# Two edits to an order of work: where a delta-rule chunk reads its old state, and how weight loads and row transposes follow each other on one queue

## The chip, the core and the metric

The kernel runs on one core of a Trainium2 chip. A core has a matrix engine (TensorE, PE in the profile; PEld is its weight load), three engines for elementwise work (VectorE = DVE, ScalarE = ACT, GpSimd = POOL) and SyncE (SP), which here does nothing but issue transfers. Each engine takes its instructions in order; semaphores join the engines. The metric is the device time of one execution in microseconds (us); lower is better.

## The reference

Three stages in a row. Only what is computed matters here:

```python
# 1. delta-rule attention, 4 x 8 heads, 768 tokens, width 48
for t in range(S):
    y[:, :, t] = q[t] @ state                       # reads the old state
    v_old = k_n[t] @ state
    state = state + beta[t] * outer(k_n[t], v[t] - v_old)
# 2. dense layer on 3072 tokens of width 384:   x = leaky_relu(x @ w_in) @ w_out      (d_ff 2048)
# 3. expert layer, 8 experts, one per token:
e_idx = argmax(x @ w_gate); gate_w = softmax(x @ w_gate)[e_idx]; eom = sigmoid(x @ w_output_gate)
out[mask_e] = gate_w * eom[e] * (relu(x[mask_e] @ w1[e]) @ w2[e])                     # d_ff 1024
```

## The kernel before, in words

**Stage one and two, woven together.** The 768 tokens are cut into 12 chunks of 64. For one chunk the loop over tokens becomes a few triangular solves. `chain(k, c)` (L299) is a generator that writes the PE, ACT and DVE work of chunk c in pieces; each `yield` ends a piece. The pieces of a chunk are: the product of the keys with the old state (L344), then three small solves in turn (`solve`, L317 to L321: 64 short fp32 products each), each followed by `take` (ACT and DVE copy the result out of PSUM and hand it to the next solve), then the state update (L380, 64 products, and a DVE addition, L389), and last the products of the attention scores with u (L328, out `y`). The output y is a sum of two parts. The part "query times old state" is written by `state_part(0)` and `state_part(1)`, 32 short products each, by way of `read` (L328). The first call of `state_part` takes the two PSUM banks of y from the pool psS, which has two banks in all; before y these banks hold the gram products of another chunk (`gram`, L77), and ACT (L123) and DVE (L128) have to copy those out first.

`weave` runs the main loop over steps n = 16 to 95, eight to a chunk. In each step PE gets, in the order in which the code writes them: one piece of `chain`; `moe1_up` (L556, 18 products of the dense layer for an earlier chunk); sometimes a gram; whatever lies in the list `k.between`; and `moe1_down` (L581, 12 products). PE, DVE and ACT keep that written order in the loop; POOL and SP are ordered by a planner. Chunk 2's chain falls in steps 15 to 22: the gram of chunk 5 (L77) is in step 17, the piece with the second solve in step 18, the third solve in step 19, the state update in step 20.

Which piece reads the old state depends on c. For chunk 1, `state_part(0)` stands before the third solve and `state_part(1)` behind the products of the state update. For even chunks from 2 on, `state_part(0)` stands before the second solve and `state_part(1)` goes into `k.between` of the step of the third solve. For odd chunks from 3 on, both go into `k.between`.

**Stage three.** The rows of stage two are scattered to DRAM by expert, and a table gives 4 slots, each with a list of 128-row tiles; tile number s uses slot s % 4. A slot owns two buffers for the weights of an expert (`wb`, 1.5 MB each). `moe2_setup` (L732) loads the first expert of each slot. A first, early tile of each slot (names with `_e`) runs inside `finish`. The main rounds are in `moe2`, with these helpers:

- `select(k, s)` (L903 to L907): SP reads two numbers of the table into registers and issues the two weight loads of the tile's slot, under a condition: the data moves only where the expert of the slot changes.
- `gather` (L892): POOL fetches the tile's rows from DRAM into `row`.
- `flip` (L900): SP issues a transfer that transposes `row` into `xT`. The first main tile is transposed by PE instead (`flip_pe`, L589, inside `finish`).
- `moe2_up` (L926, 72 products, then ACT L929 and DVE L930) and `moe2_down` (L940, 24 products, then DVE L945 and a scatter by POOL, L946).

The order on SP is written by hand here (it is the one engine that is ordered by hand in this stage): `flip` of tile 1, then `select` of tiles 0, 1, 2 and 3, then in `run`, after the down product of tile s, `flip` of tile s + 2 and `select` of tile s + 4. SP's transfers go through one hardware queue (q1).

Of the kernel before, what the change touches and what calls it, by code (L numbers as in the profile page):

```python
# [28 lines left out]
def half(i, n=64):  # L29
    return slice(64 * i, 64 * i + n)  # L30
# [264 lines left out]
def spilled(k, w):  # L295
    return w[:, : NST * D].rearrange("p (m d) -> p m d", m=NST), w


def chain(k, c):  # L299
# [17 lines left out]
    def solve(w, right, src, dst, first):  # L317
        for m in range(GM):
            for ab, s in ALL4:
                q, p, f = quarter(s, src ^ ab), quarter(s, dst ^ ab), GM * ab + m  # L320
                PE.matmul(ks[ab][p, m], w[q, f], right[q, f], start=first, stop=True, skip_group_check=True)  # L321
# [27 lines left out]
    def state_part(part):  # L349
        if not y:  # L350
            y.extend(banks())
        for i in range(NPR):
            for b in gs:
                g, m = b ^ 1 ^ part, NPR * b + i
                for p in gs:
                    read(g, p, m, old_w, GM * (g ^ p) + m, half(p ^ b, 48), t.q, part == 0 and i == 0, False)
# [3 lines left out]
    if c > 1 and c % 2:  # L360
        k.between.append(lambda: state_part(0))
    yield
    if c > 1 and c % 2 == 0:
        state_part(0)
    solve(t.lx, u, 0, 1, False)
    take(r, -1.0)
    yield
    if c == 1:
        state_part(0)
    solve(t.z, r, 1, 1, True)  # L370
    if c > 1:
        k.between.append(lambda: state_part(1))
    take(u, 1.0)
    yield
    if c < NCH - 1:
        sc, sc_w = spilled(k, k.state[c % 2])
        for m in range(GM):
            for ab, s in ALL4:
                f = GM * ab + m
                PE.matmul(ks[s][half(ab, 48), m], t.kg[half(s), f], u[half(s), f], start=True, stop=True, skip_group_check=True)  # L380
        k.fill()
        if c == 1:
            state_part(1)
        if c == 0:
            A.activation(sc[:, ms[0]], ks[0][0:112], AF.Copy)
            V.tensor_copy(sc[:, ms[1]], ks[1][0:112])
        else:
            for s in gs:
                V.tensor_tensor(sc[:, ms[s]], ks[s][0:112], old[:, ms[s]], op=ALU.add)  # L389
        k.sc = sc, sc_w  # L390
# [495 lines left out]
def gather(k, s, idx):  # L886
    t = Ctx()
    t.st = s % 4
    t.xT = None
    t.n = f"e{s}" if idx is k.ridx0 else str(s)  # L890
    t.row = k.q3.tile([128, XCOL], I32, tag="row2", name=f"row2_{t.n}")
    k.nc.gpsimd.indirect_dma_start(  # L892
        out=t.row[:, :], out_offset=None, in_=k.xd[:, :],
        in_offset=bass.IndirectOffsetOnAxis(ap=idx[:, s : s + 1], axis=0))
    return t


def flip(k, t):
    t.xT = k.q4.tile([128, 6, 128], F16, tag="xT2", name=f"xT2_{t.n}")
    k.nc.sync.dma_start_transpose(out=t.xT, in_=t.row[:, 0:384].bitcast(F16))  # L900


def select(k, s):  # L903
    e = k.nc.sync.value_load(k.wsel[0:1, 0, s : s + 1], min_val=0, max_val=7)
    need = k.nc.sync.value_load(k.wsel[0:1, 1, s : s + 1], min_val=0, max_val=1)
    for w in range(2):
        k.nc.sync.dma_start(k.wb[w][s % 4][:, :], k.wd[w][bass.ds(e * 128, 128), :], cond=need, cond_hint=False)  # L907


def moe2_up(k, t):  # L910
    nc = k.nc
    V, A, PE = nc.vector, nc.scalar, nc.tensor
    w1 = k.wb[0][t.st].rearrange("p (h a f) -> p h a f", h=2, a=3)
    if t.xT is None:
        t.xT = k.q4.tile([128, 6, 128], F16, tag="xT2", name=f"xT2_{t.n}")
        flip_pe(k, t.xT, t.row[:, 0:384].bitcast(F16), (A, V), t.n)
    t.h = [k.q2.tile([128, 8, 128], F16, tag=f"h2{i}", name=f"h2{i}_{t.n}") for i in range(2)]
    for f4 in range(2):
        ps, tag = ((k.psA, "psA"), (k.psO, f"psO{t.st % 2}"))[f4]
        hp = ps.tile([128, 4, 128], F32, tag=tag, name=f"hp2_{t.n}_{f4}")  # L920
        for ff in range(4):
            f = 4 * f4 + ff
            i = 0
            for kk in range(3):
                for l, r in PASSES:
                    PE.matmul(hp[:, ff], w1[:, l, kk, 128 * f : 128 * f + 128], t.xT[:, 3 * r + kk], start=(i == 0), stop=(i == 8))  # L926
                    i += 1
        fs = slice(4 * f4, 4 * f4 + 4)
        A.activation(t.h[0][:, fs], hp, AF.Relu)  # L929
        V.scalar_tensor_tensor(t.h[1][:, fs], hp, 0.0, t.h[0][:, fs], op0=ALU.max, op1=ALU.subtract)  # L930


def moe2_down(k, t, then=None):
    nc = k.nc
    w2 = k.wb[1][t.st].rearrange("p (h f c) -> p h f c", h=2, f=8)
    o = k.psL.tile([128, 384], F32, tag="psL", name=f"o2_{t.n}")
    i = 0
    for f in range(8):
        for l, r in PASSES:
            nc.tensor.matmul(o, t.h[l][:, f], w2[:, r, f], start=(i == 0), stop=(i == 23))  # L940
            i += 1
            if then is not None and i == 15:
                then()
    y = k.q4.tile([128, XCOL], F32, tag="y2", name=f"y2_{t.n}")[:, 0:384]
    nc.vector.tensor_scalar(y, o, t.row[:, 384:385].bitcast(F32), None, op0=ALU.mult)  # L945
    nc.gpsimd.indirect_dma_start(  # L946
        out=k.out[:, :], out_offset=bass.IndirectOffsetOnAxis(ap=t.row[:, 385:386], axis=0),
        in_=y, in_offset=None, bounds_check=3071, oob_is_err=False)


def moe2(k, ahead):
    n = 4 * NSL

    def head(s):
        select(k, s)
        return gather(k, s, k.ridx)

    def run(lo, hi, ts):
        for s in range(lo, min(lo + 4, hi)):
            if s not in ts:  # L960
                ts[s] = head(s)
                if s < lo + 2:
                    flip(k, ts[s])
        moe2_up(k, ts[lo])
        for s in range(lo, hi):
            if s + 1 < hi:
                moe2_up(k, ts[s + 1])
            moe2_down(k, ts[s])
            if s + 2 < hi:
                flip(k, ts[s + 2])  # L970
            if s + 4 < hi:
                ts[s + 4] = head(s + 4)

    flip(k, ahead[1])
    for s in range(4):
        select(k, s)
    run(0, n - 8, ahead)
    more = k.nc.values_load(k.wsel[0:1, 2, 0:1], min_val=0, max_val=8)  # L978
    with k.tc.If(more > NSL - 2):
        run(n - 8, n - 4, {})  # L980
        with k.tc.If(more > NSL - 1):
            run(n - 4, n, {})


def weave(k):
# [98 lines left out]
    nv_make(k, 0, s0)  # L1084
    nv_make(k, 1, s0)
    ch = chain(k, 0)
    run(ch)
    run(ch)
# [29 lines left out]
    sca()  # L1118
    inv(12)
    ch = chain(k, 1)  # L1120
    run(ch)
    low()
# [5 lines left out]
    for n in range(8, 16):  # L1128
# [19 lines left out]
        if s == 7:  # L1148
            ch = chain(k, 2)
            run(ch)  # L1150
            td = k.p1.tile([128, 32, 32], F32, tag="td", name="td2")
            ga = k_gram(k, 4)
            k_gram_out(k, 4, td, ga)
            flipped(k, 1, pair[1])
            z_make(k, 2, pair[1])
            z_make(k, 3, pair[1])
# [316 lines left out]
```

## Time and profile before

| what | value |
|---|---|
| median of 3 runs | 835.78 us (835.57 to 837.72) |
| profiled execution, its own time | 837.97 us |
| its span, first to last instruction | 835.7 us |
| mean granted TensorE clock in it | 0.98 |
| PE busy | 757.3 us |
| DVE, POOL, ACT busy | 479.6, 408.2, 330.4 us |

The page of the profile gives busy time by engine and in 40 slices of the span. The views behind it name each instruction by engine and line, what it writes and reads (out<-in), its start and length, and in square brackets the idle time before it and what ended that. "issue" there means that the engine waited for nothing that the profile shows. Kinds of DMA packets are listed by queue: q1 carries SP's transfers, q0 those of POOL, q8 and q14 instructions on their way to the engines.

### The profile page before, as it was taken

How to read it: one execution, taken by the hardware profiler on the slowest of the kernel's cores; microseconds unless marked ns; L12 is line 12 of the kernel's file. 1: busy time of each engine (PE TensorE's matmuls, PEld its weight loads, DVE VectorE, ACT ScalarE, POOL GpSimd, SP SyncE). 2: the span in 40 equal slices, each digit the busy share in tenths (PEclk: the TensorE clock that was granted, in tenths of full speed). 3: DMA queues.
4: the chain of work that ended last, by engine and by line, in shares of the span. 5: the costliest groups of instructions: out<-in, count | busy, mean ns of one | idle time of the engine just before them, and what ended most of it. 6: DMA issues, size and time to landing. Idle time of an engine off the chain costs nothing. (4 is left out here: it accounts for less than half of the span.)

```text
span 835.7 us, 29458 instructions
## 1 busy us (share of the span) xinstructions
PE 757.3 (91%) x12652; PEld 577.0 (69%) x12652; DVE 479.6 (57%) x1108; ACT 330.4 (40%) x653; POOL 408.2 (49%) x584
## 2 busy tenths in 40 slices
PE   5057778999999999999999999999997999999993
PEld 5045556677777777777777777777776887877881
DVE  5997986566666666667666777884462222222220
ACT  4244657234654465445634465653311111111120
POOL 1049862588478856885688635622042221222110
PEclk9997899999999999999999999999999999999997
DMA  8824336425582548263725496949727327897540
GB/s 276 295 72 147 106 120 200 132 73 162 168 232 73 163 151 247 75 161 122 227 83 136 130 304 197 325 140 375 297 70 243 87 67 209 286 301 222 166 90 12
DMA packets 100137, 145.03 MB, mean 174 GB/s; under 512 B 42321, under 2 KB 69748, under 8 KB 97187
## 3 DMA queue, kind: packets, MB, share of 16 engines
q1 hardware_dynamic: 94882, 128.10, 50.1%
q0 software_dynamic: 5120, 15.00, 5.5%
q8 instruction: 101, 1.65, 0.8%
q14 instruction: 34, 0.27, 0.1%
HBM read 152.28 MB, written 35.42 MB: 225 GB/s over the span
## 5 line engine op out<-in xcount | busy, mean ns | idle before, releaser
L556 PE MATMUL h<-xx,win 128*128 128x256 f16 x1728 | 211.9, 278 | 12.3 <-ACT ws L497 4.6
L556 PEld LDWEIGHTS <-win 128*128 128x128 f16 x1728 | 166.5, 99 | 42.1 <-issue 7.2
L581 PE MATMUL o<-wout,gh 128*128 128x384 f16 x768 | 188.4, 329 | 0.9 <-ACT gh L567 0.8
L581 PE MATMUL o<-wout,gl 128*128 128x384 f16 x384 | 125.0, 328 | 0.5 <-DVE gl L570 0.5
L926 PEld LDWEIGHTS <-wb 128*128 128x128 f16 x2016 | 114.9, 98 | 9.3 <-issue 3.9
L566 DVE SCALAR_TENSOR_TENSOR h<-h,g 128x512 f32<-128x512 f32 x96 | 66.7, 695 | 77.5 <-ACT g L563 77.0
L926 PE MATMUL hp<-xT,wb 128*128 128x128 f16 x1728 | 100.2, 219 | 4.4 <-DMA xT<-row 2.5
L563 ACT ACTIVATE g<-h 128x512 f32<-128x512 f32 x96 | 57.3, 597 | 118.1 <-PE h L556 114.3
L930 DVE SCALAR_TENSOR_TENSOR h<-hp,h 128x512 f16<-128x512 f32 x48 | 33.2, 692 | 122.1 <-ACT h L929 122.1
L581 PEld LDWEIGHTS <-gh 128*128 128x128 f16 x768 | 71.6, 98 | 44.0 <-issue 1.7
L570 DVE TENSOR_TENSOR gl<-h,gh 128x512 f16<-128x512 f32 x96 | 66.3, 691 | 55.1 <-ACT gh L567 54.1
L940 PE MATMUL o<-wb,h 128*128 128x384 f16 x576 | 97.3, 326 | 0.0
L946 POOL DMA_INDIRECT out_dram<-y,row x24 | 24.0, 998 | 146.0 <-DVE y L945 131.1
L529 POOL TENSOR_SCALAR we<-we 128x512 f32<-128x512 f32 x35 | 52.8, 1509 | 83.8 <-ACT whl L525 61.5
L929 ACT ACTIVATE h<-hp 128x512 f16<-128x512 f32 x48 | 28.7, 597 | 160.6 <-PE hp L926 160.6
L567 ACT ACTIVATE gh<-h 128x512 f16<-128x512 f32 x96 | 57.3, 597 | 81.1 <-DVE h L566 80.9
L226 POOL TENSOR_TENSOR x<-x,tmp 128x30 f32<-128x30 f32 (+9 forms) x150 | 81.3, 542 | 11.6
L224 POOL TENSOR_TENSOR tmp<-x 128x30 f32<-128x30 f32 (+9 forms) x150 | 78.5, 523 | 10.3
L940 PEld LDWEIGHTS <-h 128*128 128x128 f16 x576 | 55.4, 98 | 34.3
L525 ACT ACTIVATE whl<-we 128x512 f16<-128x512 f32 x96 | 56.6, 623 | 4.0 <-DMA wd<-whl 3.2
L581 PEld LDWEIGHTS <-gl 128*128 128x128 f16 x384 | 37.7, 98 | 26.5 <-DVE gl L570 1.5
L532 DVE SCALAR_TENSOR_TENSOR whl<-we,whl 128x512 f16<-128x512 f32 x61 | 50.9, 855 | 6.1 <-ACT whl L525 6.0
(267 smaller groups left out, 954.0 us busy)
## 6 DMA issues: line engine op xcount, KB each, us to landing
wb<-wd SPq DMA_DIRECT2D x56, 1536.0 KB
we<-in_we_dram SPq DMA_DIRECT2D x96, 256.0 KB
wd<-whl SPq DMA_DIRECT2D x96, 256.0 KB
kc<-in_kt_dram SPq DMA_DIRECT2D x24, 224.0 KB
q<-in_qt_dram SPq DMA_DIRECT2D x24, 224.0 KB
nv<-in_kv_dram SPq DMA_DIRECT2D x12, 384.0 KB
kn<-in_kv_dram SPq DMA_DIRECT2D x12, 384.0 KB
w<-in_win_dram SPq DMA_DIRECT2D x6, 512.0 KB
```

Of the source, the lines that this page charges most:

```text
L224: E.tensor_tensor(tv, x[:, q, j : j + 1].to_broadcast([128, n, j]), x[:, j : j + 1, 0:j].to_broadcast([128, n, j]), op=ALU.mult)
L226: k.after = E.tensor_tensor(x[:, q, 0:j], x[:, q, 0:j], tv, op=ALU.add)
L525: nc.scalar.activation(hl[:, 0], w32, AF.Copy, scale=sc)
L529: nc.gpsimd.tensor_scalar(w32, w32, sc, None, op0=ALU.mult)
L556: PE.matmul(hp[:, ff], k.win[l][:, f, kk], xx[:, r, kk], start=(n == 0), stop=(n == 8))
L563: A.activation(g32, hp, AF.Copy, scale=0.01 * 2.0**-10)
L566: V.scalar_tensor_tensor(hp, hp, 2.0**-10, g32, op0=ALU.mult, op1=ALU.max)
L567: k.mark = A.activation(gh, hp, AF.Copy)
L570: k.mark_gl = V.tensor_tensor(gl, hp, gh, op=ALU.subtract)
L581: k.mark_down = k.nc.tensor.matmul(k.o[t], gg[l][:, ff, 128 * t : 128 * t + 128], k.wout[r][:, f], start=(f == 0 and i == 0), stop=(f == N ...
L926: PE.matmul(hp[:, ff], w1[:, l, kk, 128 * f : 128 * f + 128], t.xT[:, 3 * r + kk], start=(i == 0), stop=(i == 8))
L940: nc.tensor.matmul(o, t.h[l][:, f], w2[:, r, f], start=(i == 0), stop=(i == 23))
```

## The change

In `chain`, chunk 2 is treated as chunk 1 was: `state_part(0)` stands before the third solve (step 19) and no longer before the second (step 18), and `state_part(1)` stands behind the products of the state update (step 20) and no longer in `k.between` of step 19. The other chunks keep their places. In `moe2`, SP's opening order is now `select` 0, `flip` 1, `select` 1, `flip` 2, `select` 2, `flip` 3, `select` 3; and `run` leaves out a `flip` that has been made.

```diff
@@ chain @@
-    if c > 1 and c % 2 == 0:
+    if c > 2 and c % 2 == 0:
         state_part(0)
     solve(t.lx, u, 0, 1, False)
     take(r, -1.0)
     yield
-    if c == 1:
+    if c in (1, 2):
         state_part(0)
     solve(t.z, r, 1, 1, True)
-    if c > 1:
+    if c > 2:
         k.between.append(lambda: state_part(1))
     take(u, 1.0)
     yield
...
         k.fill()
-        if c == 1:
+        if c in (1, 2):
             state_part(1)
@@ moe2 @@
             moe2_down(k, ts[s])
-            if s + 2 < hi:
+            if s + 2 < hi and ts[s + 2].xT is None:
                 flip(k, ts[s + 2])
             if s + 4 < hi:
                 ts[s + 4] = head(s + 4)
 
-    flip(k, ahead[1])
     for s in range(4):
         select(k, s)
+        if s < 3:
+            flip(k, ahead[s + 1])
     run(0, n - 8, ahead)
```

## Rows read from the trace of the kernel before

**Rows 1.** Page, part 1: busy us of an engine, share, instructions.

```profile
PE 757.3 (91%) x12652; PEld 577.0 (69%) x12652; DVE 479.6 (57%) x1108; ACT 330.4 (40%) x653; POOL 408.2 (49%) x584
```

**Rows 2.** PE's waits, 100 to 150 us: who, for whom, total us, times, longest.

```profile
PE y L328 <- ACT td L123: 2.6, 1, 2.6
...
PE h L556 <- issue: 2.0, 1, 2.0
...
PE y L328 <- DVE td L128: 0.2, 1, 0.2
```

**Rows 3.** PE's longest group of waits from 155 to 620 us.

```profile
PE y L328 <- ACT td L123: 0.9, 3, 0.5
```

**Rows 4.** PE's waits from 620 us to the end.

```profile
PE hp L926 <- DMA xT<-row: 2.5, 1, 2.5
PE hp L926 <- DMA wb<-wd: 1.9, 1, 1.9
```

**Rows 5.** PE's timeline, steps 18 and 19: start, length, work, [idle before].

```profile
144.59 0.33 PE L328 MATMUL y<-q,state 48*64 48x64 f32 x4 [2.60 <-ACT td L123]
...
149.73 1.15 PE L556 MATMUL h<-xx,win 128*128 128x256 f16 x8 [1.96 <-issue]
150.68 0.85 PE L581 MATMUL o<-wout,gh 128*128 128x384 f16 x2
...
154.33 0.88 PE L321 MATMUL ks<-r,z 32*32 32x48 f32 x64
155.14 2.14 PE L556 MATMUL h<-xx,win 128*128 128x256 f16 x18
157.21 0.69 PE L328 MATMUL y<-q,state 48*64 48x64 f32 x32
157.84 0.50 PE L581 MATMUL o<-wout,gh 128*128 128x384 f16 x2
...
159.89 0.94 PE L380 MATMUL ks<-u,kn 64*48 64x48 f32 x64
```

**Rows 6.** DVE's timeline: the operand of the second solve; the copy that frees psS.

```profile
139.26 0.55 DVE L315 TENSOR_SCALAR u<-ks 128x384 f32<-128x384 f32 x1
...
143.22 1.71 DVE L128 COPY td<-ga 32x256 f32<-32x256 f32 x4
```

**Rows 7.** DMA packets by kind, 138.5 to 147.3 us: count, MB, busy share.

```profile
q1 hardware_dynamic: 2833, 1.95, 84.7%
```

**Rows 8.** The same, 147.3 to 149.8 us.

```profile
q8 instruction: 1, 0.02, 2.4%
```

**Rows 9.** Stretch; busy of PE, PEld, DVE, ACT, POOL; granted clock; DMA share, GB/s.

```profile
149.80:154.00 4.20, 4.20 (x19) 2.38 (x19) 1.73 (x3) 2.23 (x4) 2.90 (x12) 0.59 0.30 80
```

**Rows 10.** PE's timeline, first main tiles of the expert layer.

```profile
628.86 4.19 PE L926 MATMUL hp<-xT,wb 128*128 128x128 f16 x72 [1.91 <-DMA wb<-wd]
...
636.79 4.18 PE L926 MATMUL hp<-xT,wb 128*128 128x128 f16 x72
...
647.39 4.18 PE L926 MATMUL hp<-xT,wb 128*128 128x128 f16 x72 [2.52 <-DMA xT<-row]
```

**Rows 11.** SP's timeline, 560 to 660 us.

```profile
625.56 1.29 SPq L900 DMA_TRANSPOSE xT<-row  x1
628.73 7.34 SPq L907 DMA_DIRECT2D wb<-wd  x8
636.25 1.47 SPq L900 DMA_TRANSPOSE xT<-row  x1
...
640.01 3.59 SPq L900 DMA_TRANSPOSE xT<-row  x1
```

**Rows 12.** DVE's timeline: the table that `select` reads is ready.

```profile
616.64 0.36 DVE L869 CAST t_wsel<-t_idE 128x32 int32<-128x32 f32 x1
```

**Rows 13.** SP's issues of weight loads, 628.5 to 634 us: ns min/median/max.

```profile
L907 SPq DMA_DIRECT2D wb<-wd x6: 73/73/109, 628.7 to 633.4; - x6
```

**Rows 14.** The same, 634 to 636.1 us.

```profile
L907 SPq DMA_DIRECT2D wb<-wd x2: 343/348/353, 635.0 to 635.7; - x2
```

## The prediction

> **What bounds the kernel now.** I read the page's busy times first: PE works 757.3 of 835.7 us [rows 1], so a change pays where PE stands still, and only there. So the next view is PE's waits, stretch by stretch. Around chunk 2 it lists 2.6 us for the copy of `td` by ACT, 0.2 for that by DVE and 2.0 in which nothing visible is missing ("issue") [rows 2]. From 155 to 620 us its largest entry is 0.9 us in three waits [rows 3]. After 620 us there are two waits: 2.5 us for a transposed row and 1.9 for a weight load [rows 4]. The reader is to see that PE has next to no pause behind either place, so time won there reaches the end, as long as what feeds PE moves up too. Last come the timelines of PE, DVE and SP at the two places.
>
> **Where the times stand.** The sum is made in the profiled execution: 837.97 us, that is its span of 835.7 and 2.27 around it. The median of the runs shown is 835.78, 2.19 below that time; I take the sum off both alike.
>
> **Part 1, SP's order in the expert layer.** Before, SP issues the transposition of tile 1 at 625.56, when the rows of that tile are there, then eight weight loads from 628.73 to 636.07, then the transposition of tile 2 at 636.25 [rows 11]. Tile 0 waits for the first of those loads: PE stands 1.91 us until 628.86 [rows 10]. Yet that load moves nothing: the first six issues take 73 to 109 ns, the last two 343 and 353 [rows 13, 14]; I read the long ones as loads whose condition holds, 1.5 MB each, so only slot 3 loads. Tile 2's transposition then stands behind these 3 MB in the one queue: issued at 636.25, it lets PE go at 647.39, 11.1 us later, and PE has stood 2.52 us by then [rows 10, 11].
>
> After, `select` 0 comes first. The table that it reads is ready at 617.0 [rows 12], and the early tile of slot 0 is long done, so it runs in the time in which SP waited for rows anyway. Tile 0 starts at 626.95, where the product before it ends (628.86 less 1.91): 1.91 us are gone. SP goes on as before at its own pace: a `select` costs 1.9 us until its first load (628.73 less 626.85) and 0.4 more, a transposition 1.3 [rows 11]. That gives: tile 1's transposition 625.56 as before; `select` 1 at 628.7; tile 2's at 629.4; `select` 2 at 632.6; tile 3's at 633.2; `select` 3 with the real loads at 636.4, 1.4 us later than now. PE needs them as follows. A tile takes 7.93 us (636.79 less 628.86) [rows 10], so tiles 1, 2 and 3 start at 634.9, 642.8 and 650.7. Tile 2's transposition has 13.4 us, more than the 11.1 that it took behind the 3 MB, so even the worst row leaves no wait: 2.52 us are gone. Tile 3's has 17.5 us. Slot 3's first load has 14.3 us; before, it had landed, by the queue's order, by the time the transposition behind it did, 12.4 us after its issue at 635.03. So its cost is 0, with 1.9 us to spare; without that cover it is what the load is late. Tile 4's transposition now follows `select` 4 and 5 directly; it waits, as before, only for slot 1 to come free at 642.8, and has 15 us. Nothing is added on PE, POOL, ACT or DVE. **Part 1: -4.43 us.** Its bounds are -1.9 (the transposition is as late as now relative to its use) and -4.5.
>
> **Part 2, chunk 2's old-state product.** PE ends step 17 at 141.99 (144.59 less 2.60) and then stands, because the first product of `state_part(0)` writes a psS bank that ACT and DVE are still copying from; DVE is done at 144.93 [rows 5, 6]. After, the second solve stands there. Its operand was ready at 139.81 [rows 6], so PE goes on: solve 0.81 (155.14 less 154.33), `moe1_up` 2.07 (157.21 less 155.14), `moe1_down` 2.05 (159.89 less 157.84) [rows 5], which ends step 18 at 146.9. By then the banks are free for `state_part(0)`, which costs 0.63 in one run (157.84 less 157.21). The moved pieces cost the same at their new places, and the state update's DVE addition depends on the products before `state_part(1)`, not on it.
>
> The "issue" pause decides how much of that lasts. PE stops at 147.77 in the middle of `moe1_up`, ten products in, and goes on at 149.73 [rows 5]. From 138.5 to 147.3 no instruction packet appears, while SP's queue keeps the DMA engines 85% busy; the next packet, one of 0.02 MB, comes in the stretch from 147.3 to 149.8 [rows 7, 8]. I read it as PE's next block of instructions, late behind SP's traffic. That traffic was issued before PE's standstill and does not change, so my likeliest case keeps the block's time. PE then has the same 106 products to do until it runs dry (32 + 64 + 10 before; 64 + 18 + 12 and 12 of the 32 of `state_part(0)` after). It runs dry at 147.2 and waits until 149.73: 2.5 us instead of 1.96. What is left of step 19 is 0.40 + 0.81 + 2.07 + 2.05. [...] Step 20 then starts at 156.7 with 0.63 of `state_part(1)` still to do, against 159.89 without: 159.89 - 156.7 - 0.63 = 2.6. **Part 2: -2.6 us.** Bounds: 0, if the block comes later by what was won, and -6.8, if PE finds no pause and no half clock at all (step 20 at 152.5: 159.89 - 152.5 - 0.63). In an execution that has no such pause to begin with, it is the standstill alone, 2.60 + 0.16 and the 0.3 by which the interrupted product took longer: -3.1, close to the value taken.
>
> ACT and DVE must follow a step of 4.9 us instead of 12. Step 19 shows that they can: it takes 5.6 us (159.89 less 154.33) [rows 5] without a wait of PE.
>
> [...]
>
> **Sum.** -4.43 - 2.6 = -7.0: the profiled execution would take 831.0 us, the median 828.8.
>
> **The rivals.**
> *A. The block is not held by the traffic; PE asks for it late.* Then the shorter run of short products between wide ones gives it time, and pause and half clock go. For it: the pause follows 96 short products in a row. Against: nearly nine microseconds without a packet, which begin while PE works. Part 2 is -6.8, the sum -11.2: 824.6. [...]
> *B. Part 2 is given back*: the block comes later by what PE won, or ACT and DVE, with td and the norms of chunks 4 and 5 in step 18, hold PE in step 19. For it: DVE's copy ends at 144.93, three us into the new step 18 [rows 6], and the norms follow it. Against: the operand of the third solve is due only at 147.5, and a late block would give both engines more time. Only part 1 is left: 831.4.
> *C. Part 1 is given back*: slot 3's loads, now 1.4 us later and shared with two transpositions, are late for tile 3. For it: the DMA engines are full then. Against: the 1.9 us to spare. With 4.4 us late, 833.2.
> *D. Slower.* In step 20, 64 products of the state update and 32 of `state_part(1)` now stand in a row, as before the pause at 147.77. If a block is late there by as much as the packet-free stretch [rows 7], 8.8 us, PE holds some 7 us of it and loses 1.6 to the half clock: +8.6, so 837.4. It decides from a hold of 5.4 us on. Against: the only pause of this kind is 2.0 us long.
>
> **Chances.** The forecast 0.56, A 0.13, B 0.14, C 0.09, D 0.04, other mixtures 0.04. The range reaches to A below and short of C above: 824.5 to 832.5. A measurement of this kernel can tell 0.3%, 2.5 us, from no change: faster means under 833.3. The forecast, A and B lie there, and most of C's weight is at its edge: faster 0.86, the same 0.10, slower 0.04.
>
> **What would show it.** After: no wait of PE for `xT` or `wb` in the main rounds; the first main tile starts right behind the last early product; tile 2's and 3's transpositions are issued before the two long L907 issues; tile 3 starts without a wait. In step 18 the solve L321 follows L581 with no gap; a pause "issue" of about 2.5 us stands in or before `state_part(0)` of step 19, and ends after a packet of q8. Wrong would be: that pause gone (A), or a new wait of PE for gl, r or u in steps 18 to 20 (B), for `wb` at tile 3 (C), or "issue" of many microseconds in step 20 (D).

## The result, and the profile after

The changed kernel takes 825.62 us (median of 5 runs, 825.37 to 826.13) beside 835.57 for the kernel before (835.02 to 837.72) on the same chip: a ratio of 0.9862, interval 0.9841 to 0.9883. It is faster by about 10 to 11.5 us. The forecast was 828.8: right in sign, too small in size by 3 to 4.5 us. Rival A's 824.6 is nearest.

The profiled execution of after took 825.53 us, its span 823.7 (before: 837.97 and 835.7). The two views of PE's waits of after, 100 to 150 us and 620 us to the end (who, for whom, total us, times, longest):

```profile
PE h L556 <- DVE gl L570: 4.2, 1, 4.2
PE h L556 <- ACT ws L497: 1.5, 1, 1.5
PE o L581 <- ACT gh L567: 1.4, 1, 1.4
PE h L556 <- POOL win L499: 0.6, 1, 0.6
PE o L581 <- DVE gl L570: 0.2, 1, 0.2
```

```profile
PE hp L926 <- DVE xT L594: 0.2, 1, 0.2
```

Gone are the waits for td and "issue" [rows 2] and those for `xT` and `wb` [rows 4]; what is listed up to 150 us ends by 121.84, ahead of step 18 (141.06). PE's timeline of after, steps 18 to 20 (start, length, work, [idle before]):

```profile
141.06 0.88 PE L321 MATMUL ks<-u,lx 32*32 32x48 f32 x64
141.87 2.14 PE L556 MATMUL h<-xx,win 128*128 128x256 f16 x18
...
145.89 0.70 PE L328 MATMUL y<-q,state 48*64 48x64 f32 x32
146.52 0.88 PE L321 MATMUL ks<-r,z 32*32 32x48 f32 x64
147.33 2.14 PE L556 MATMUL h<-xx,win 128*128 128x256 f16 x18
...
151.35 0.94 PE L380 MATMUL ks<-u,kn 64*48 64x48 f32 x64
152.11 0.67 PE L328 MATMUL y<-q,state 48*64 48x64 f32 x32
```

No pause stands in it. From the end of step 17 to the state update it is 10.29 us (151.35 less 141.06); before it was 17.90 (159.89 less 141.99) [rows 5]. Of the 7.6 us won, `state_part(1)` at 152.11 takes 0.6 back: part 2 is worth -7.0 in this pair of traces. Windows of after (columns as in [rows 9]; the granted clock is the first lone number behind the five engines) and its DMA packets by kind, 138.5 to 147.3 us:

```profile
146.00:148.00 2.00, 2.00 (x103) 1.80 (x103) 1.86 (x3) 0.07 (x1) 1.52 (x3) 1.00 0.58 142
148.00:150.00 2.00, 2.00 (x19) 1.61 (x17) 1.45 (x3) 2.00 (x5) 1.57 (x5) 1.00 0.78 259
150.00:152.00 2.00, 2.00 (x65) 1.29 (x67) 1.53 (x3) 0.86 (x2) 1.59 (x6) 1.00 0.50 162
```

```profile
q1 hardware_dynamic: 2785, 1.86, 92.2%
q8 instruction: 2, 0.03, 1.5%
```

The granted clock is 1.00 in all three windows, and two instruction packets arrive while q1 is at least as busy as before (92.2% for the 84.7% of [rows 7]). So the half clock [rows 9] went too, and a busy q1 alone didn't keep packets out here.

Now part 1. SP's and PE's timelines of after:

```profile
610.94 0.54 SPq L907 DMA_DIRECT2D wb<-wd  x2
617.72 1.28 SPq L900 DMA_TRANSPOSE xT<-row  x1
620.79 0.52 SPq L907 DMA_DIRECT2D wb<-wd  x2
621.49 1.27 SPq L900 DMA_TRANSPOSE xT<-row  x1
624.94 0.52 SPq L907 DMA_DIRECT2D wb<-wd  x2
625.64 1.33 SPq L900 DMA_TRANSPOSE xT<-row  x1
628.53 7.39 SPq L907 DMA_DIRECT2D wb<-wd  x6
```

```profile
614.69 4.06 PE L940 MATMUL o_e<-wb,h_e 128*128 128x384 f16 x24
618.59 0.50 PE L589 MATMUL tp<-cmat,row 128*128 128x128 f16 x6
619.50 0.27 PE L926 MATMUL hp<-xT,wb 128*128 128x128 f16 x2 [0.41 <-ACT xT L592]
619.92 4.07 PE L926 MATMUL hp<-xT,wb 128*128 128x128 f16 x70 [0.15 <-DVE xT L594]
...
643.57 1.61 PE L926 MATMUL hp<-xT,wb 128*128 128x128 f16 x26
```

All of it now runs 7.84 us earlier (tile 1's transposition at 617.72 for 625.56). From the last early work (619.09, that is 619.50 less 0.41) to tile 3's start it is 24.5 us; before it was 28.4 (626.95 to 647.39 + 7.92) [rows 10]. Part 1 is worth -3.9. The two parts make 10.9 of the 12.0 us between the spans; 0.9 is that step 17 ended earlier in this execution, ahead of both edits.

### The profile page after: what moved, and what is told of

Same layout as the page of the kernel before. It is cut to its first block, busy times and chain, and to the rows that moved or that the text cites. A ratio compares the mean times of both kernels' runs of the same rounds, so it can differ in the third digit from the quotient of the medians.

```text
span 823.7 us, 29462 instructions
## 1 busy us (share of the span) xinstructions
PE 750.9 (91%) x12652; PEld 572.8 (70%) x12652; DVE 480.0 (58%) x1108; ACT 329.8 (40%) x653; POOL 407.2 (49%) x584
## 5 line engine op out<-in xcount | busy, mean ns | idle before, releaser
L940 PE MATMUL o<-wb,h 128*128 128x384 f16 x576 | 97.4, 326 | 0.0
L224 POOL TENSOR_TENSOR tmp<-x 128x30 f32<-128x30 f32 (+9 forms) x150 | 76.2, 508 | 10.2
L940 PEld LDWEIGHTS <-h 128*128 128x128 f16 x576 | 55.4, 98 | 34.3
```

Source lines behind the costliest of these rows:

```text
L224: E.tensor_tensor(tv, x[:, q, j : j + 1].to_broadcast([128, n, j]), x[:, j : j + 1, 0:j].to_broadcast([128, n, j]), op=ALU.mult)
```

## The experiments

Three theories were set up once the result was known. **S**: PE's standstill at the psS bank is the cause; a block of instructions that is outstanding when PE comes to stand arrives only after PE goes on, and the half clock follows from the lack of work. **T**, the forecast's: SP's traffic holds the block. **R**, rival A's reason: a long run of short products makes PE ask late. The runs fall into three groups, each on a chip of its own; each group has its own runs of the kernel before, with medians of 848.07, 838.09 and 850.43 us. Differences are taken within a group.

### First group: one part at a time

**Chain alone.** The edit is the diff's part in `chain`, with `moe2` as before.

```diff
-    if c > 1 and c % 2 == 0:
+    if c > 2 and c % 2 == 0:
...
-        if c == 1:
+        if c in (1, 2):
```

> Only the edit in chain (chunk 2's state_part calls one step later); SP's order as before. Theory 1 (PE's issue asks for no block of instructions while it stands at a wait, so the pause 'issue' in step 18 is a child of the standstill for psS): standstill, pause and half clock all go, 6 to 7 us below the kernel before, no PE wait of the kind 'issue' in steps 18 to 20. Theory 2 (the forecast: the block is late because of SP's traffic and keeps its time): 2.6 us below, with a pause of about 2.5 us in step 19.

Measured: 841.4 us, ratio 0.9931 (0.9911 to 0.9950), -5.8 us. The only wait of PE from 125 to 160 us, and the packets from 138.5 to 147.3:

```profile
PE ga L77 <- issue: 0.8, 1, 0.8
```

```profile
q1 hardware_dynamic: 2767, 1.83, 92.7%
q8 instruction: 2, 0.03, 2.0%
```

The 0.8 us come before step 18. Part 2 alone is worth more than twice the -2.6 forecast, under the old SP order and full traffic.

**SP's order alone.** The edit is the diff's part in `moe2`, with `chain` as before.

```diff
-    flip(k, ahead[1])
     for s in range(4):
         select(k, s)
+        if s < 3:
+            flip(k, ahead[s + 1])
```

> Only the edit in moe2 (SP's select and flip alternate); chain as before. Both theories: the waits of PE for wb (1.9) and xT (2.5) go, 3.9 to 4.4 us below the kernel before; standstill and pause of step 18 stay. Rival: the gain of the whole change is more than the sum of its parts; then this run and e1 together fall short of the 10 us by over 1.

Measured: 847.2 us, ratio 0.9991 (0.9975 to 1.0007): nothing, against 4 us expected. The standstill (1.3 us) and the pause (2.6) of step 18 stay, as expected. On this chip ACT halts between the two halves of an early tile's `h_e`. In the run with the chain alone, so with the old SP order, ACT's and PE's timelines show it ("remote": released by something that the trace doesn't name):

```profile
628.49 0.60 ACT L929 ACTIVATE h_e<-hp_e 128x512 f16<-128x512 f32 x1 [8.09 <-remote]
```

```profile
629.15 4.11 PE L940 MATMUL o_e<-wb,h_e 128*128 128x384 f16 x12 [5.40 <-issue]
633.05 4.69 PE L926 MATMUL hp<-xT,wb 128*128 128x128 f16 x72
```

PE stands 5.4 us for it, SP's queue catches up meanwhile, and the first main tile finds `wb` and `xT` without a wait. With SP's order alone the hold is there too:

```profile
637.02 4.11 PE L940 MATMUL o_e<-wb,h_e 128*128 128x384 f16 x12 [5.70 <-ACT h_e L929]
```

From the end of the hold to the end of the span it is 208.8 us with the old order (837.9 less 629.15) and 208.9 with the new one (845.9 less 637.02). So part 1 has nothing to win where another hold covers it. What holds ACT there stays open. The two halves together (-6.6) fall short of the 10 us of the whole change by over 1, the sign that the expectation set for a gain beyond the sum; the whole was not run on this chip, and the second group has the sum on one chip.

**More products ahead.** 64 (half) or 128 (full) short products are added ahead of chunk 2's chain, to shift where a block ends against the standstill; they clear sums in `ks`, so chunk 2's result is not the reference's. In the kernel before q8 brings 63 packets from 155 to 600 us, and PE does 8,077 products and 8,066 weight loads, 256 of both to a packet: the block of the two expectations. Their store is what PE has at hand without a packet: from 138.5 to 147.3 us, where none appears [rows 7], it does 184 products and 182 weight loads.

```diff
+    if c == 2:
+        for i in range(64):      # full: 128
+            PE.matmul(ks[i % 2][:, 0, 0:8], k.ident, k.cmat[:, 0, 0:8], start=True, stop=True, skip_group_check=True)
```

> The kernel before with 64 more products of 8 columns on PE (128 instructions, half a block of 256) in the first piece of chunk 2, 1.6 us of added work whose result is overwritten. Theory 1: the standstill for psS stays near 2.6 us, but no block falls due in it, so the pause (2.0) and the half clock (1.6) go: 2 us below the kernel before. Theory 2 (traffic) and theory 3 (the 96 short products in a row run the store dry): standstill and row of products are as before, the pause stays: 1.6 us above.

> As e4 with 128 such products (256 instructions, one whole block), 3.2 us of added work. Theory 1: blocks fall due at the same places as in the kernel before, so the pause and the half clock are back: 3.2 us above the kernel before and about 5 above e4. Theories 2 and 3: 1.6 above e4.

Measured: 846.79 us (0.9987, 0.9970 to 1.0004) and 850.14 (1.0019, 1.0003 to 1.0035). Both show a standstill of 1.7 + 0.2 us and no pause; the second expectation, that the pause comes back, missed; the first run's time fits theory 1 (-2.0) and not the others (+1.6). In the second trace a packet of q8 had come (146.5 us) before PE stood (from 147.9); for the first this isn't shown. After the standstill the first ran at half clock (its solve, L321, took 1.50 us), the second did not (0.88).

### Second group: the sum, and the cause

**The changed kernel again, and SP's order again.** The edits are the whole diff, and its part in `moe2` as above.

> The changed kernel itself, for the sum beside its halves on one chip. If the ratio first measured (0.986) is the change's and not that chip's: 0.985 to 0.988, about -10 to -12 us, with no wait of PE for xT or wb and no issue pause in steps 18 to 20. On a chip where ACT is held between the halves of an early tile's h, SP's queue has time to catch up and part 1 has less to win: then -6 to -8 us (0.991 to 0.993).

> SP's order alone, on another chip. Where ACT is not held in the early tiles the kernel before waits 1.9 us for wb and 2.5 for xT, and this one not: -3.5 to -4.4 us (0.995 to 0.996). Where ACT is held by more than 5 us, the kernel before has next to no such waits and this is worth 0 (0.999 to 1.001). In both cases the standstill for psS in step 18 stays and an issue pause of about 2 us with it.

Measured: the changed kernel 826.92 us, ratio 0.9869 (0.9846 to 0.9892), -11.0; SP's order alone 833.31, ratio 0.9941 (0.9922 to 0.9960), -4.9. So part 1 is real where ACT isn't held, and about -6 is left for part 2. The waits that part 1 removes do stand on this chip under the old order: 1.9 us for `wb` and 2.7 to 3.0 for `xT` in the traces of the two runs that follow. SP's order alone taught more than that. PE's timeline and windows of SP's order alone:

```profile
145.01 0.33 PE L328 MATMUL y<-q,state 48*64 48x64 f32 x4 [2.50 <-ACT td L123]
145.51 0.71 PE L328 MATMUL y<-q,state 48*64 48x64 f32 x28 [0.17 <-DVE td L128]
146.15 1.50 PE L321 MATMUL ks<-u,lx 32*32 32x48 f32 x64
147.58 3.03 PE L556 MATMUL h<-xx,win 128*128 128x256 f16 x18
```

```profile
146.00:148.00 2.00, 2.00 (x78) 1.66 (x70) 0.26 (x1) 0.24 (x1) 1.92 (x2) 0.51 0.79 255
148.00:150.00 2.00, 2.00 (x13) 1.52 (x12) 1.90 (x5) 0.25 (x1) 0.42 (x1) 0.64 0.28 99
```

The old standstill is there and no "issue" pause (a packet had come before 142.3, contrary to the expectation). Yet the granted clock falls to 0.51 over 146 to 148 us: the solve takes 1.50 us for 0.88, `moe1_up` 3.03 for 2.14. So the half clock can follow the standstill with no late block, and costs 1.5 us here.

**A longer wait for ACT.** ACT copies its half of chunk 5's td three times.

```diff
-        for _, dst, blk in td_blocks(c, td, ga, ab):
-            k.nc.scalar.activation(dst, blk, AF.Copy)
+        for _ in range(3 if c == 5 else 1):
+            for _, dst, blk in td_blocks(c, td, ga, ab):
+                k.nc.scalar.activation(dst, blk, AF.Copy)
```

> The kernel before, in which ACT copies its half of chunk 5's td three times instead of once, so that PE stands about 3 us longer at the psS bank (some 5.5 us, till about 147.6). Theory S (a block of PE's instructions that is outstanding when PE comes to stand is fetched only after PE goes on): the packet comes some 3 us after PE goes on, near 150.5, and the issue pause of about 2 us and the half clock stay: +2.5 to +3.5 us. Theory T (the block is held by SP's traffic and comes at its own time, near 147.4): it is there when PE needs it, no issue pause and no half clock by it; the 3 us are paid out of the pause of 2 and the 1.6 of the half clock: -1 to +0.5 us.

Measured: 840.18 us, ratio 1.0024 (1.0008 to 1.0040). The packet came near 147.3 and there is no pause, as T would have it. But PE ran four products at 144.61, ahead of its second wait, so S can count from there, though the packet then came about where PE's second standstill (145.09 to 147.34) ended; and the clock is at 0.50 from 144.5 us on. The time lies between what the two expected, and the run doesn't decide between them.

**No standstill, all else in place.** The gram of chunk 5 stands in step 16, so the banks are free when `state_part(0)` comes in step 18, at its old place.

```diff
-            c = a if odd and s == 5 else p + 3 if not odd and s == 0 and p > 2 else 5 if n == 17 else NCH
+            c = a if odd and s == 5 else p + 3 if not odd and s == 0 and p > 2 else 5 if n == 16 else NCH
```

> The kernel before, with the gram of chunk 5 one step earlier (step 16 for 17), so that its psS banks are copied out by the time state_part(0) of chunk 2 wants them in step 18: the old-state product stays where it was, 96 short products in a row, and only the standstill goes. Theory S: no standstill, no issue pause, no half clock after it: -5.5 to -6.8 us. Theory T (traffic): PE runs dry earlier and waits for the same packet till about 149.7: 0 us, with an issue pause of 4 to 5 us. Theory R (the run of short products makes PE ask late): the pause of 2 us and the half clock stay, only the standstill's 2.8 us are won.

Measured: 834.34 us, ratio 0.9956 (0.9937 to 0.9975), -3.7 us, less than the -5.5 to -6.8 of S. PE's timeline:

```profile
142.96 0.69 PE L328 MATMUL y<-q,state 48*64 48x64 f32 x32
143.58 0.88 PE L321 MATMUL ks<-u,lx 32*32 32x48 f32 x64
144.40 2.14 PE L556 MATMUL h<-xx,win 128*128 128x256 f16 x18
...
148.42 0.88 PE L321 MATMUL ks<-r,z 32*32 32x48 f32 x64
```

The 96 short products in a row are as before, and neither pause nor half clock follows: R falls, and T's pause of 4 to 5 us is absent. Steps 18 to 20 are as short as in after, within 0.2 us once `state_part(1)` is counted alike. Part of the timed shortfall is 0.9 us of new waits in step 17 of this trace. The rest may lie in what it is held against: from the end of step 17 (142.96) to the state update (153.98) it is 11.02 us; in SP's order alone, the execution on this chip without the pause, it is 15.55 (142.51 to 158.06), and 15.55 - 11.02 - 0.9 = 3.6. Which kind the timed executions were is not on record.

### Third group: the deciding run

**Standstill on both engines.** As the longer wait, but DVE copies its half three times too, so that nothing runs until 147.8.

```diff
-            for _, dst, blk in td_blocks(c, td, ga, ab):
-                k.nc.vector.tensor_copy(dst, blk)
+            for _ in range(3 if c == 5 else 1):
+                for _, dst, blk in td_blocks(c, td, ga, ab):
+                    k.nc.vector.tensor_copy(dst, blk)
```

> The kernel before, in which ACT and DVE both copy their halves of chunk 5's td three times, so that no product of state_part(0) can run before about 147.5 to 148 (one standstill of 5.5 to 6 us without the four products that ran at 144.6 in the run with ACT's copies alone). Theory S (an outstanding block of instructions comes only after PE goes on): where the block is not there before 142, its packet comes 1.5 to 3 us after PE goes on, at 149 to 151, and PE pauses at issue near 151. Theory T (SP's traffic holds the block): the packet comes near 147.4 again, where SP's burst ends, and there is no issue pause. In both the granted clock is 0.5 from the standstill on for some 6 us, and step 19 starts at 154.5 to 157: +0.5 to +4 us.

Measured: 852.93 us, ratio 1.0030 (1.0010 to 1.0049). PE's timeline, then the DMA packets in two stretches, 148 to 149.6 and 149.6 to 149.9 us:

```profile
147.76 0.48 PE L330 MATMUL y<-q,state 48*64 48x64 f32 x4 [5.76 <-ACT td L124]
148.70 1.12 PE L330 MATMUL y<-q,state 48*64 48x64 f32 x28 [0.45 <-DVE td L130]
149.74 1.50 PE L323 MATMUL ks<-u,lx 32*32 32x48 f32 x64
```

```profile
DMA packets 0, 0.00 MB, mean 0 GB/s; under 512 B 0, under 2 KB 0, under 8 KB 0
```

```profile
q8 instruction: 1, 0.02, 23.9%
```

SP's traffic is over by 148, no queue moves anything for 1.6 us, and still the block is not there; its packet comes 1.9 us after PE went on. T, which put it near 147.4, falls; the timing is S's. The windows (columns as above) show the clock go down while PE still stands, between 146.8 and 147, and stay there:

```profile
144.50:146.00 1.50, 0.00 (x0) 0.00 (x0) 1.39 (x4) 1.40 (x5) 0.00 (x0) 1.00 0.89 305
146.50:146.80 0.30, 0.00 (x0) 0.00 (x0) 0.27 (x2) 0.28 (x2) 0.00 (x0) 1.00 0.27 106
147.00:147.50 0.50, 0.00 (x0) 0.00 (x0) 0.47 (x2) 0.48 (x2) 0.00 (x0) 0.50 0.72 275
148.00:150.00 2.00, 1.55 (x46) 1.27 (x48) 0.52 (x2) 0.37 (x1) 1.49 (x1) 0.50 0.04 8
```

S's pause near 151 didn't come: at half clock PE took longer over the products that it had left.

S isn't a rule either. The traces of before and of after have an earlier standstill, of 3.24 and 3.33 us, in which a packet comes (at 77.2 and 76.8 us) while PE stands. In the kernel before PE stands from 75.78 to 79.02; its timeline, and the packets from 77.2 to 77.3:

```profile
79.02 1.50 PE L321 MATMUL ks<-u,lx 32*32 32x48 f32 x64 [3.24 <-ACT u L311]
```

```profile
q8 instruction: 1, 0.02, 71.8%
q1 hardware_dynamic: 5, 0.01, 58.6%
```

This packet waited neither for PE nor for q1 to fall quiet, and the solve behind the standstill ran at half clock (1.50 us, granted clock 0.50 from 78.9 to 82.2); in after the same solve took 0.88 us at 1.00. So the runs show that the standstill of step 18 brings the costs behind it, not by what mechanism the block came late.

**Second half of the move alone.** Only `state_part(1)` of chunk 2 moves, to step 20.

```diff
-    if c > 1:
+    if c > 2:
         k.between.append(lambda: state_part(1))
...
-        if c == 1:
+        if c in (1, 2):
             state_part(1)
```

> Of part 2 only the second half: state_part(1) behind the state update of step 20, state_part(0) left before the second solve of step 18. If the standstill at the psS bank is what costs, nothing changes: 32 products stand in step 20 and no longer in step 19, the wait of 2.6 us for td stays, and an issue pause or a half clock of about 1.5 us after it. 0.998 to 1.002. If the second half's move were worth something by itself (a shorter step 19), -0.6 us or more.

Measured: 849.59 us, ratio 0.9976 (0.9959 to 0.9992), -0.7 to -3.5 us, a little more than expected. Its trace has the standstill (1.3 us) and a pause of 2.55, as expected; where the gain comes from stays open.

**One step further.** In the changed kernel, PE's six transposing products (`tp`) had slipped behind the last early down product, and the first main tile waited 0.41 + 0.15 us for their copies. Here they are held inside it.

```diff
-    moe2_down(k, ts[3], first)
+    with k.tc.manual_schedule(engines={mybir.EngineType.PE}):
+        moe2_down(k, ts[3], first)
```

> The changed kernel with PE's six transposing products of the first main tile held inside the down product of the last early tile, after its 16th product, as the program writes them, and not behind it. The waits of PE for the copies of xT (0.41 + 0.15 us) go, as ACT and DVE copy beside the last eight products: -0.5 us against the changed kernel, so 0.986 against the kernel before on a chip where the changed one has 0.9869. A measurement can't tell 0.5 us; the waits in the trace can.

Measured: 842.55 us, ratio 0.9888 (0.9871 to 0.9906). The two waits are gone from the trace, but ACT's hold, 7.5 us here, stands in the same place. It beats the kernel before by 9.5 us by the ratio, 7.9 by the medians; that it beats the changed kernel isn't shown. From the hold's end to the end of the span it takes 209.4 us (840.3 less 630.95), near the 208.8 and 208.9 of the first group, so all of it is won ahead of the hold. Why the ratio gives more than part 2's -5.8 stays open.

## Why the prediction was right or wrong

**Part 1 was right**: -4.43 forecast, -3.9 in the traces, -4.9 (-3.4 to -6.5) timed alone. SP's order came out as worked out: counted from tile 1's transposition, the next issues were forecast 3.1, 3.8, 7.0, 7.6 and 10.8 us later and came 3.1, 3.8, 7.2, 7.9 and 10.8 later. Tile 3 starts without a wait, so the 1.9 us to spare held and rival C is out. Missed: that the first main tile starts right behind the early product. The planner's order on PE was taken as fixed, and its change costs 0.56 us. That another hold can cover part 1 wasn't foreseen.

**Part 2 failed at one step**: "That traffic was issued before PE's standstill and does not change, so my likeliest case keeps the block's time", and with it the 1.6 us for the half clock that its 156.7 holds: 3.65 us for the 12 products of `moe1_down` behind the pause (154.33 less 150.68) less 2.05 for those of step 19 (159.89 less 157.84) [rows 5, 9]. The term, -2.6, measured -7.0 in the pair of traces and -5.8 (-4.2 to -7.5) timed alone. The rows allowed two readings: no packet from 138.5 to 147.3 goes with SP's traffic [rows 7], but also with PE's standstill from 141.99 to 144.59 [rows 5], which lies within it. The forecast took the first. The chain alone (two packets under the same traffic), the gram moved ahead (no standstill, no pause, full clock) and the standstill on both engines (no packet with the queues empty) speak for the second. Of the eight traces with the standstill in step 18, three show the pause (1.96, 2.6 and 2.55 us), and of the seven whose windows reach past it six have a stretch at a granted clock of 0.50 between 144 and 154 us. Of the five without it none shows the pause in steps 18 to 20, and the three read further (after, the chain alone, the gram moved ahead) have every solve there at 0.88 us. So the pause and the half clock hung on the standstill and were not costs of their own; the edit that took the first took all.

**Also wrong** was the value for executions without the pause, -3.1, "the standstill alone". SP's order alone shows such an execution, and the half clock is in it: its way from the end of step 17 to the state update is 15.55 us, 5.3 over that of after; less 0.6 for `state_part(1)`, part 2 is worth -4.7 there. The timed -5.8 lies between this and -7.0.

**Rival A** had the price (-6.8) and half of the reason: that the traffic doesn't hold the block fits the standstill on both engines, but the run of short products is innocent (the gram moved ahead). B, C and D did not come: steps 19 and 20 show no wait of PE, so ACT and DVE follow the shorter steps.

**What stays open**: why a block is outstanding at the standstill in some executions and there in others, why it came only after PE went on in step 18 when another came while PE stood at 77.2 us, and why one standstill of 1.9 us (full) brought no half clock when another of 1.9 (half) did.

## What to carry to other kernels

When a wait, an unexplained "issue" pause and a stretch of half clock stand in a row on one engine (here 2.76, 1.96 and 3.4 us), price them first as one chain whose first link pays for all, and only then as separate costs. A stretch with no instruction packet had two suspects here, the queues and the engine itself: look at whether the engine stood, and test each by an edit of its own. And a saving in a queue's order may count only where nothing else gives that queue time to catch up: SP's order alone won 4.9 us without ACT's hold and nothing (0.9991) with it.

## What the runs showed of the hardware

- No packet of q8 came from 138.5 to 149.6 us, over a standstill that ended at 147.76; the next came 1.9 us after PE went on, with the DMA queues empty for 1.6 us before it (standstill on both engines). That is no rule: in the kernel before a packet came at 77.2 us, in the middle of a standstill from 75.78 to 79.02.
- The granted clock fell from 1.00 to 0.50 within 1.1 us after a standstill of 2.7 us (SP's order alone, second group), during one of 5.8 (both engines, 0.9 us before PE went on), and after one of 1.9 (half, 0.77 over 148 to 150 us, then 0.50); after another of 1.9 (full) it stayed at 1.00. In step 18 of the kernel before it fell only after the pause (0.50 from 150.5 to 153.9 us) [rows 5, 9]: the solve behind its standstill of 2.76 us still ran at full clock (0.88 us).
- In every trace of the first and third group PE stood 5.4 to 7.5 us ahead of an early tile's L940, in five for ACT's `h_e`, in two (the chain alone, the second half) with "issue" named; for the chain alone ACT's own timeline shows it held 8.09 us there. In the traces of before, of after and of the second group no such wait appears.
